# Where the value products and a fill step stand in an attention round on TensorE

## The chip, the cores and the metric

The kernel runs on one NeuronCore of one Trainium2 chip. The metric is the device time of one execution in microseconds (us). Before the change the median of three runs is 2140.48 us (2140.02 to 6885.32).

## The reference

Two blocks follow each other. Attention with 4 sequences, 8 heads, 768 positions and head size 64; each position sees the 128 latest positions and the first 4 ("sinks"). Its output, reshaped to 3072 tokens by 512, goes through 8 experts whose weights come from a Sinkhorn normalisation over all tokens.

```python
scores = scale * np.matmul(q, k.transpose(0, 1, 3, 2))
keep = is_sink | in_window
scores = np.where(keep, scores, -1000000000.0)
a = np.exp(scores - np.max(scores, axis=-1, keepdims=True))
a = a / (np.sum(a, axis=-1, keepdims=True) + 1e-09)
attn = np.matmul(a, v)                      # -> x: 3072 x 512
P = np.exp(x @ w_gate - max); 8 x (rows, columns normalised)
for e in range(E):
    out += P[:, e:e + 1] * (np.maximum(x @ w1[e], 0.0) @ w2[e])
```

## The kernel before, in words

Attention is cut into 48 units: sequence b, block i of 128 query positions (6 per sequence), and half hh of the heads (4 heads, which are two pairs pr = 0, 1). A unit passes through a pipeline of rounds (the loop at L719). In round n TensorE works on four units at once, and on two other things:

- **Scores** of unit n+1 (`scores`, L451): per pair six matmuls, two heads in turn, into one PSUM bank per head (`st0` to `st3`). VectorE adds the mask and takes the maximum (L471), ScalarE takes the exponential (L474), VectorE makes the reciprocal of the sum (L475, L476), GpSimd scales (L478).
- **Values** of unit n-1 (`values`, L511): per pair up to seven matmuls into `O` (L527): three for each of the two key blocks and one for the sinks. After pair 1, `store_x` (L531) copies `O` to `xr`, one half on ScalarE and one on VectorE (both L539), and after hh = 1 stores it.
- **Transposition of q and k** of unit n+2 (`transpose_qk`, L424): four transposes into `st0` (L433), then a high part on ScalarE (L437, `KQ`) and the rest on VectorE (L438, `KQ`).
- **Transposition of the probabilities** of unit n (`transpose_p`, L480): four transposes per pair (two in the first block of a sequence) into `st1` for pair 0 and `st2` for pair 1 (L489). `split` (L348, its instructions have L350) makes the high part `PT` on ScalarE and then the rest on VectorE. The bank is free when VectorE has read it. **Sinks** (`transpose_sinks`, L494) are transposed into `st3` (L506) and copied on ScalarE (L508).
- A **gate step** (`gate_step`): a piece of the logits of tokens that are finished. For the first 1024 tokens this is a group of eight and sixteen matmuls (L568, L577); after that it is one matmul of `gate_tile` (L557), the last of which is followed by a copy on VectorE (L560).
- A **fill step** (`run_fill(1)`, from round 5 on): a piece of the first expert's products. One piece is half of a first product (L606, six matmuls; every second one is followed by L611 on ScalarE and L612 on VectorE) or a part of a second product (L622, three matmuls; at times followed by L628 on ScalarE).

The order on TensorE is written out by hand (`manual_schedule` for TensorE alone); the order of the other engines' queues is set by the tile framework's scheduler from dependencies and program order. Since `st0` to `st3` are one bank each and serve scores, q and k, probabilities and sinks in turn, the scores of pair 0 in the next round (banks `st0`, `st1`) wait for VectorE's reading of the transposed q and k and of pair 0's probabilities, and the scores of pair 1 (`st2`, `st3`) for VectorE's reading of pair 1's probabilities and ScalarE's reading of the sinks.

The kernel's rest (some 1850 us of it) is expert products, which depend on the attention stage's results.

Of the kernel before, what the change touches and what calls it, by code (L numbers as in the profile page):

```python
# [229 lines left out]
def tile_sink_attention_moe(ctx: ExitStack, tc: tile.TileContext, q, k, v, wg, w1, w2, out):  # L230
# [23 lines left out]
    def f32(ap):  # L254
        return ap.bitcast(F32)
# [52 lines left out]
    def split_gate():  # L308
        for kc in range(KC):
            nc.vector.tensor_copy(wgr[:, kc, :], zero)  # L310
        nc.vector.tensor_copy(wgr[:, :, 0:E], wg_raw)
        nc.vector.tensor_sub(wgr[:, :, E:2 * E], wg_raw, f32(wgr[:, :, 0:E]))
        nc.vector.tensor_add(sel, ident[0:2 * E, 0:E], ident[0:2 * E, E:2 * E])
# [54 lines left out]
    def st_tile(shape, k=None):  # L368
        if k is None:
            k, turns[0] = turns[0] % 4, turns[0] + 1  # L370
        return ps_st.tile(shape, F32, name=f"st{k}")
# [30 lines left out]
    def load_sinks(b):  # L402
        vs = seq[b] = att.tile([SK, D], F32, name="vs")
        for r0 in range(0, SK, NK):
            (nc.sync if b else nc.scalar).dma_start(vs[r0:r0 + NK, :], v[b, :, 0:SINK, :])

    def split_sinks(b):

        vm = att1.tile([SK, H, D], F32, name="vm")
        nc.gpsimd.tensor_tensor(vm, seq[b].unsqueeze(1).broadcast_to([SK, H, D]), bd.unsqueeze(2).broadcast_to([SK, H, D]), op=ALU.mult)  # L410
        VS = seq[b] = att.tile([SK, H * D], F32R, name="VS")
        vmf = vm.rearrange("p h d -> p (h d)")
        nc.gpsimd.tensor_scalar(VS, vmf, 1.0, 1.0, op0=ALU.mult, op1=ALU.mult)
        nc.gpsimd.tensor_sub(VS[2 * NK:], vmf[2 * NK:], f32(VS[2 * NK:]))

    def load_block(b, i):
        raws[b, i] = r = [att.tile([P, H, D], F32, name=nm) for nm in ("kr", "qr", "vr")]
        cuts = (0, HH, H) if (b, i) == (0, 0) else (0, H)
        for ts in (((r[0], k), (r[1], q)), ((r[2], v),)):
            for h0, h1 in zip(cuts, cuts[1:]):  # L420
                for t, src in ts:
                    nc.sync.dma_start(t[:, h0:h1, :], src[b, h0:h1, i * P:(i + 1) * P, :].rearrange("h p d -> p h d"))

    def transpose_qk(n):  # L424

        b, i, hh = units[n]
        us[n] = {}
        kr, qr, _ = raws[b, i]
        h0 = hh * HH
        pt = st_tile([P, 4, P], 3 if n == 1 else 0)  # L430
        for pr in range(NP):
            for j, r in enumerate((kr, qr)):
                nc.tensor.transpose(pt[:, 2 * pr + j, :], r[:, h0 + 2 * pr:h0 + 2 * pr + 2, :].rearrange("p h d -> p (h d)"), ident)  # L433
        t = KQ[hh]
        hi, lo = (t[:, w, :, SINK:].rearrange("p r (a c) -> p r a c", a=2)[:, :, :, turn_of(b, i)] for w in range(2))
        src = pt.rearrange("p (r a) t -> p r a t", a=2)
        nc.scalar.copy(hi, src)  # L437
        nc.vector.tensor_sub(lo, src, f32(hi))  # L438
        if i == 1:

            nc.vector.tensor_copy(t[:, :, :, 0:SINK], f32(t[:, :, :, place(b, 0)])[:, :, :, 0:SINK])

    def split_v(n):
        b, i, hh = units[n]
        V = att.tile([P, 2, HH * D], F32R, name="V", bufs=5)
        vs = raws[b, i][2][:, hh * HH:(hh + 1) * HH, :].rearrange("p h d -> p (h d)")
        nc.gpsimd.tensor_scalar(V[:, 0], vs, 1.0, 1.0, op0=ALU.mult, op1=ALU.mult)
        nc.gpsimd.tensor_sub(V[:, 1], vs, f32(V[:, 0]))
        us[n]["V"] = V
# [30 lines left out]
    def transpose_p(n, pr):  # L480

        b, i, hh = units[n]
        u = us[n]
        sc = u["sc"]
        ws = (1,) if i == 0 else (0, 1)
        t = st_tile([P, len(ws), 2, P], 1 + pr)
        for j, w in enumerate(ws):
            for h in range(2):
                nc.tensor.transpose(t[:, j, h, :], sc[:, 2 * pr + h, place(b, i + 1 - w)], ident)  # L489
        PT = att.tile([P, 2, len(ws), 2, P], F32R, name="PT", bufs=5)  # L490
        u["split"] = split(PT, t)
        u["PT", pr] = PT
# [18 lines left out]
    def values(n, pr):  # L511

        b, i, hh = units[n]
        u = us[n]
        if pr == 0:
            u["O"] = ps_o.tile([P, NP, 2, P], F32, name="O")
        cs = slice(pr * P, (pr + 1) * P)
        ops = []
        ws = (1,) if i == 0 else (0, 1)
        for j, w in enumerate(ws):  # L520
            V = us[n - 2 + 2 * w]["V"]
            for x_, y_ in ((0, 0), (0, 1), (1, 0)):
                ops.append((V[:, x_, cs], u["PT", pr][:, y_, j]))
        if i:
            ops.append((seq[b][:, hh * HH * D:][:, cs], u["PS"].unsqueeze(1).broadcast_to([SK, 2, P])))
        for j, (x_, y_) in enumerate(ops):
            nc.tensor.matmul(u["O"][:, pr], lhsT=x_, rhs=y_, start=(j == 0), stop=(j == len(ops) - 1))  # L527
        if pr == NP - 1:
            store_x(n)

    def store_x(n):  # L531
        b, i, hh = units[n]
        u = us[n]
        O = u["O"]
        quads = [(slice(r * D, (r + 1) * D), O[r * D:(r + 1) * D, :, r, :]) for r in range(2)]
        tok = b * S + i * P
        xr = u["xr"] = us[n - 1]["xr"] if hh else att.tile([P, KC, P], F32, name="xr")
        for (rows, o), cp_ in zip(quads, (nc.scalar.copy, nc.vector.tensor_copy)):
            cp_(xr[rows, hh * NP:(hh + 1) * NP, :], o)  # L539
        if hh == 1:  # L540
            nc.sync.dma_start(xscr[:, :, tok:tok + P].rearrange("k p t -> p k t"), xr)
            if tok < NPART:
                g, cols = tok // GT, slice(tok % HT, tok % HT + P)
                for kh in range(2):
                    x_ = xr[:, kh * KH:(kh + 1) * KH, :]
                    b_ = xblock(kh, tok // HT)
                    nc.scalar.copy(b_[:, 0, :, cols], x_)
                    nc.gpsimd.tensor_sub(b_[:, 1, :, cols], x_, f32(b_[:, 0, :, cols]))
                if (tok + P) % GT == 0:
                    later.append(gate_group(g))  # L550
            else:
                later.append(gate_tile(tok // P, xr))
# [28 lines left out]
    def gate_step():  # L581
        if gates and next(gates[0], 0) == 0:
            gates.pop(0)
            gate_step()
# [76 lines left out]
    def run_fill(k_):  # L661
        for _ in range(k_):
            next(fill, None)
# [54 lines left out]
    with tc.manual_schedule(engines={PE}):  # L718
        for n in range(-2, L + 3):  # L719
            on = lambda j: 0 <= j < L  # L720
            if on(n + 2):
                b, i, hh = units[n + 2]
                if hh == 0:
                    with (tc.high_priority() if n == -2 else nullcontext()):
                        load_block(b, i)
                    if i == 0:
                        load_sinks(b)
            if n == -2:
                nc.sync.dma_start(wg_raw, wg.rearrange("(k p) e -> p k e", p=P))
            if n == 2:  # L730
                with tc.issue_after(us[1]["split"][1]):
                    split_gate()
            gates += later
            later.clear()
            if on(n + 1):
                scores(n + 1, 0)
                scores(n + 1, 1)
            if on(n - 1):
                values(n - 1, 0)
            if n >= START:  # L740
                run_fill(1)
            gate_step()
            for j in (0, 1) if n == -2 else (n + 2,) if n >= 0 else ():
                if on(j):
                    transpose_qk(j)
            if on(n):
                transpose_p(n, 0)
                with (tc.issue_after(us[n - 1]["scaled"]) if n > 1 else nullcontext()):
                    split_v(n)
            gate_step()  # L750
            if on(n):
                transpose_p(n, 1)
            if on(n - 1):
                values(n - 1, 1)
            gate_step()
            if on(n) and units[n][1]:
                transpose_sinks(n)
            if on(n) and units[n][1:] == (0, 1):
                with tc.issue_after(us[n]["scaled"]):
                    split_sinks(units[n][0])  # L760
            if n >= START:
                run_fill(1)
            first_w1(n)
        while gates:
            gate_step()
# [760 lines left out]
```

## Time and profile before

| what | before |
|---|---|
| median of the runs | 2140.48 us |
| the profiled execution, its own time | 2140.46 us |
| its span, first to last instruction | 2138.7 us |
| attention rounds in the trace | from about 6 to 300 us |
| granted TensorE clock, mean | 0.997 |

How to read the rows of this document: PE is TensorE, PEld its weight loads, DVE is VectorE, ACT is ScalarE, POOL is GpSimd, SP the queue that issues most DMAs. A row of the timeline gives the start in us from the span's start, the time that it took, engine, source line, operation, what it writes and reads, and how many follow each other; in square brackets the idle time before it and what ended it. A matmul's recorded time covers its whole way through the array, so that matmuls overlap in the record; from one group's start to the next group's start is what a group costs in TensorE's line.

### The profile page before, as it was taken

What the parts mean: (1) busy time and instruction counts of PE and PEld (TensorE: products, weight loads), DVE (VectorE), ACT (ScalarE), POOL (GpSimd) and SP (SyncE); (2) the same over time, 40 slices, a digit from 0 to 9 for tenths busy, and PEclk for the clock granted to TensorE, in tenths of its full rate; (3) what the DMA queues carried; (4) which work ended last, traced back from release to release, by engine and by line L of the source; (5) the groups of instructions that cost most, each with busy time, mean ns of one, the idle gap of its engine ahead of it and who ended that gap; (6) DMA issues with size and microseconds to landing.
All of it is one profiled execution on the core that took longest, in us unless ns stands there. A gap on an engine that the chain in (4) does not pass through costs nothing.

```text
span 2138.7 us, 31819 instructions
## 1 busy us (share of the span) xinstructions
PE 2120.3 (99%) x10501; PEld 1769.8 (83%) x10501; DVE 1538.8 (72%) x2821; ACT 881.9 (41%) x1867; POOL 750.4 (35%) x950
## 2 busy tenths in 40 slices
PE   8999999999999999999999999999999999999998
PEld 7898897888888888888888888888888888888887
DVE  8878868877777776766666666666657666666666
ACT  7777745444444444442333223332333223332322
POOL 7766643233232331232223222233323232233223
PEclk9999999999999999999999999999999999999999
DMA  7434326999999987686666666667866666666662
GB/s 184 95 84 101 86 80 230 314 307 312 294 309 293 310 290 251 216 282 205 204 192 201 208 192 205 203 200 262 297 204 196 199 207 194 200 207 189 205 197 85
DMA packets 397643, 453.83 MB, mean 212 GB/s; under 512 B 99680, under 2 KB 265760, under 8 KB 396576
## 3 DMA queue, kind: packets, MB, share of 16 engines
q1 hardware_dynamic: 397080, 451.57, 68.0%
q8 instruction: 86, 1.41, 0.3%
q14 instruction: 85, 0.70, 0.1%
q10 hardware_dynamic: 392, 0.16, 0.0%
HBM read 314.17 MB, written 137.46 MB: 211 GB/s over the span
## 4 chain that ended last, share of the span: by engine, by line
PE 94%; DVE 3%; ACT 1%; DMA 1%; issue 0%; POOL 0%; SPq 0%; ACTq 0%; DVEq 0%
PE c L791 40%; PE o L1350 20%; PE held L1350 8%; PE held L1035 7%; PE o L1035 7%; PE O L527 3%; PE st L468 2%; PE st L489 1%; PE o L622 1%; PE g L606 1%; ACT sc L474 1%; PE st L433 1%; DVE sc L471 0%; PE O L557 0%; PE st L606 0%
## 5 line engine op out<-in xcount | busy, mean ns | idle before, releaser
L817 ACT CAST hf<-w 128x512 fp32r<-128x512 f32 x448 | 265.0, 620 | 561.5 <-POOL w L1317 299.2
L1350 PE MATMUL o<-hf,W2q 128*128 128x512 f32 x1920 | 472.0, 389 | 0.0
L1350 PEld LDWEIGHTS o<-hf,W2q 128*128 128x128 f32 x1920 | 360.0, 188 | 75.5 <-DVE acc L1364 0.8
L791 PE MATMUL c<-T,W1q 128*128 128x512 f32 x1530 | 389.0, 389 | 0.2 <-DVE w L1298 0.2
L818 DVE TENSOR_TENSOR hf<-w,hf 128x512 fp32r<-128x512 f32 x448 | 330.4, 766 | 74.3 <-ACT hf L817 66.8
L791 PEld LDWEIGHTS c<-T,W1q 128*128 128x128 f32 x1530 | 286.7, 188 | 60.9 <-DVE w L1298 1.2
L1364 DVE TENSOR_TENSOR acc<-o,acc 128x512 f32<-128x512 f32 x298 | 204.6, 687 | 171.5 <-PE o L1350 171.5
L791 PE MATMUL c<-B,W1q 128*128 128x512 f32 x1134 | 278.3, 389 | 0.0
L1317 POOL TENSOR_TENSOR w<-w 128x512 f32<-128x512 f32 x64 | 82.7, 1292 | 493.2 <-DVE w L1299 486.6
L791 PEld LDWEIGHTS c<-B,W1q 128*128 128x128 f32 x1134 | 212.5, 188 | 44.0
L1298 DVE TENSOR_TENSOR w<-c,M 128x512 f32<-128x512 f32 x192 | 132.3, 689 | 138.8 <-PE c L791 133.1
L1294 ACT COPY M<-c 128x512 f32<-128x512 f32 x192 | 112.7, 587 | 250.4 <-PE c L791 250.3
L1350 PE MATMUL held<-hf,W2q 128*128 128x512 f32 x768 | 194.8, 389 | 0.0
L791 PE MATMUL c<-T,W1f 128*128 128x512 f32 x672 | 171.2, 390 | 0.2
L1035 PE MATMUL held<-W2f,h 128*128 128x512 f32 x672 | 171.1, 390 | 0.0
L1035 PE MATMUL o<-W2f,h 128*128 128x512 f32 x672 | 170.6, 389 | 0.1
L1350 PEld LDWEIGHTS held<-hf,W2q 128*128 128x128 f32 x768 | 144.0, 188 | 29.9
L1332 POOL TENSOR_TENSOR w<-w 128x512 f32<-128x512 f32 x64 | 105.7, 1651 | 176.2 <-DVE hf L818 176.2
L1035 PEld LDWEIGHTS o<-W2f,h 128*128 128x128 f32 x672 | 126.0, 188 | 27.0 <-DVE acc L1042 0.9
L791 PEld LDWEIGHTS c<-T,W1f 128*128 128x128 f32 x672 | 125.7, 188 | 27.1 <-ACT M L998 0.5
L1035 PEld LDWEIGHTS held<-W2f,h 128*128 128x128 f32 x672 | 125.8, 188 | 26.4 <-DVE W2f L818 0.5
L844 POOL TENSOR_TENSOR r<-r 128x256 f32<-128x256 f32 x27 | 20.1, 744 | 359.6 <-ACT M L998 210.0
(216 smaller groups left out, 3100.3 us busy)
## 6 DMA issues: line engine op xcount, KB each, us to landing
W2q<-w2s SPq DMA_DIRECT2D x448, 256.0 KB, 3.2
W1q<-w1s SPq DMA_DIRECT2D x444, 256.0 KB, 2.8
w1s<-W1f SPq DMA_DIRECT2D x56, 896.0 KB, 7.6
w2s<-WT SPq DMA_DIRECT2D x136, 256.0 KB, 3.4
r<-in_moe_w_dram SPq DMA_DIRECT2D x64, 512.0 KB, 4.0
w2s<-W2f SPq DMA_DIRECT2D x56, 256.0 KB, 4.8
PB<-psd SPq DMA_DIRECT2D x16, 512.0 KB, 4.2
w2s<-W2f SPq DMA_DIRECT2D x56, 128.0 KB, 6.5
```

Source lines behind the costliest of these rows:

```text
L468: nc.tensor.matmul(ps[h], lhsT=Q[r0:r0 + D, a, pr, :], rhs=K[r0:r0 + D, c, pr, :], start=(j == 0), stop=(j == 2))
L527: nc.tensor.matmul(u["O"][:, pr], lhsT=x_, rhs=y_, start=(j == 0), stop=(j == len(ops) - 1))
L791: nc.tensor.matmul(ps, lhsT=w1(a, k), rhs=x[:, b, k, :], start=(start and j == 0), stop=(stop and j == len(TERMS) - 1), skip_group_check=n ...
L817: nc.scalar.copy(dst[:, 0], src)
L818: at(1, lambda: nc.vector.tensor_sub(dst[:, 1], src, f32(dst[:, 0])))
L1035: nc.tensor.matmul(o, lhsT=h[c, th][:, a, off:off + P], rhs=W2F[n][:, w, c, :], start=(begin and c == 0 and j == 0), stop=(end and c == 1 ...
L1294: nc.scalar.copy(t, T["c2"])
L1298: nc.vector.tensor_add(w, T["c1"], T[m])
L1317: nc.gpsimd.tensor_sub(S3, T["A11"], T["A21"])
L1332: at(k, lambda: nc.gpsimd.tensor_sub(T["A11"], w, T["A11"]))
L1350: nc.tensor.matmul(o, lhsT=W2Q[part, n, m][:, a, k * P:(k + 1) * P], rhs=F[part, n, H_OF[m]][:, w, :], start=(j == 0 and (begin or not hol ...
L1364: nc.vector.tensor_add(sums[m, k], o, sums[m, k])
```

## The change

In the loop over rounds, three things move. Both value products of unit n-1 are now issued together, right behind the scores (before, pair 1's stood behind the transposes of the probabilities). The transposition of q and k comes next, and the first fill step and the first gate step, which stood ahead of it, come behind it. The third gate step, which stood ahead of the sinks, comes behind them. No instruction is added or removed.

```diff
             if on(n - 1):
                 values(n - 1, 0)
+                values(n - 1, 1)
+            for j in (0, 1) if n == -2 else (n + 2,) if n >= 0 else ():
+                if on(j):
+                    transpose_qk(j)
             if n >= START:
                 run_fill(1)
             gate_step()
-            for j in (0, 1) if n == -2 else (n + 2,) if n >= 0 else ():
-                if on(j):
-                    transpose_qk(j)
             if on(n):
                 transpose_p(n, 0)
...
             if on(n):
                 transpose_p(n, 1)
-            if on(n - 1):
-                values(n - 1, 1)
-            gate_step()
             if on(n) and units[n][1]:
                 transpose_sinks(n)
...
+            gate_step()
             if n >= START:
                 run_fill(1)
```

TensorE, in a round of the fourth sequence (of the kind with one gate matmul), from the end of the q and k transposes to the next round's first score matmul. `st_3749` and `st_3760` are the banks of the probabilities of pair 0 and pair 1, `st_3790` that of a score. Before:

```order
L433 MATMUL st_3742<-ident,qr 128x128
L489 MATMUL st_3749<-ident,sc 128x128 x4
L489 MATMUL st_3760<-ident,sc 128x128 x4
L527 MATMUL O<-PT,V 128x256 x6
L527 MATMUL O<-PS,VS 128x256
L506 MATMUL st_3781<-ident,SS_170 96x128
L622 MATMUL o<-W2f,h_2790 128x512 x3
L468 MATMUL st_3790<-KQ_174 128x260
```

The same place after the change (the banks of the probabilities are now `st_3759` and `st_3770`); seven value products (L527) stand no longer between the probabilities' transposes and the next scores, and a fill step (L606) and a gate step (L557) stand between q and k's transposes and theirs:

```order
L433 MATMUL st_3742<-ident,qr 128x128
L606 MATMUL g_3639<-B_131,W_3614 128x256 x2
L606 MATMUL g_3639<-B_130,W_3614 128x256 x2
L606 MATMUL g_3639<-B_131,W_3614 128x256 x2
L557 MATMUL O<-wg_raw,xr 128x8
L489 MATMUL st_3759<-ident,sc 128x128 x4
L489 MATMUL st_3770<-ident,sc 128x128 x4
L506 MATMUL st_3781<-ident,SS_170 96x128
L622 MATMUL o<-W2f,h_2804 128x512 x3
L468 MATMUL st_3790<-KQ_174 128x260
```

The seven L527 that have left this stretch stand right behind the scores now, with the other seven.

VectorE in the same round, from the last reciprocal of the softmax to the first mask and maximum (L471) of the next round. Before:

```order
L476 RECIPROCAL st<-st 128x2
L612 SCALAR_TENSOR_TENSOR h_3621<-g_3622,h_3621 128x256
L438 TENSOR_TENSOR KQ_174<-st_3742,KQ_174 128x2x2x128
L350 TENSOR_TENSOR PT<-st_3749,PT 128x512
L350 TENSOR_TENSOR PT<-st_3760,PT 128x512
L539 COPY xr<-O 64x256
L471 ISA sc,st<-st_3790,mask_79 128x260
```

After:

```order
L476 RECIPROCAL st<-st 128x2
L539 COPY xr<-O 64x256
L438 TENSOR_TENSOR KQ_174<-st_3742,KQ_174 128x2x2x128
L612 SCALAR_TENSOR_TENSOR h_3638<-g_3639,h_3638 128x256
L560 COPY Xt<-O 128x8
L350 TENSOR_TENSOR PT<-st_3759,PT 128x512
L350 TENSOR_TENSOR PT<-st_3770,PT 128x512
L471 ISA sc,st<-st_3790,mask_79 128x260
```

The copy of `O` (L539) has moved from behind the two splits of the probabilities (L350) to ahead of q and k's split (L438); the gate's copy (L560), which stood ahead of the last reciprocals, stands ahead of the splits. ScalarE's line changes in the same way: its copy of `O` now stands between the exponentials and q and k's cast, where it stood behind the casts of the probabilities.

## The prediction

> **What bounds the kernel now.** First the page, for its span and the busy times, then the busy time by stretches of 30 us.
>
> ```profile
> span 2138.7 us, 31819 instructions
> PE 2120.3 (99%) x10501; PEld 1769.8 (83%) x10501; DVE 1538.8 (72%) x2821; ACT 881.9 (41%) x1867; POOL 750.4 (35%) x950
> ```
>
> ```profile
> 0.00:30.00 30.00, 23.38 (x124) 18.46 (x125) 25.57 (x97) 19.74 (x60) 23.49 (x65) 0.89 0.78 193
> 210.00:240.00 30.00, 29.75 (x251) 26.16 (x251) 25.31 (x91) 22.33 (x71) 21.30 (x49) 1.00 0.42 98
> 240.00:270.00 30.00, 29.19 (x245) 25.85 (x244) 25.83 (x88) 22.65 (x72) 19.51 (x44) 1.00 0.33 81
> ```
>
> The columns behind the stretch's length are PE, PEld, DVE, ACT, POOL, then the granted clock. TensorE is busy almost always, also in the rounds of attention, but a matmul's row covers its way through the array, and a wait can hide under the row of the matmul ahead of it. VectorE has 25.3 us of work in 30 us there, so it is a close second. What ends the waits must therefore be read from one round, by the starts of TensorE's groups. This is a round with one gate matmul in which no weight is split:
>
> ```profile
> 212.97 0.97 PE L527 MATMUL O<-PT,V 128*128 128x256 f32 x6
> 213.90 0.87 PE L606 MATMUL g<-B,W 128*128 128x256 f32 x6
> 214.61 0.28 PE L557 MATMUL O<-wg_raw,xr 128*128 128x8 f32 x2
> 214.75 0.31 PE L433 MATMUL st<-ident,kr 128*128 128x128 f32 x1
> 214.98 1.92 POOL L478 TENSOR_SCALAR sc<-sc,st 128x260 f32<-128x260 f32 x4 [2.01 <-ACT sc L474]
> 215.22 1.04 PE L489 MATMUL st<-ident,sc 128*128 128x128 f32 x8
> 215.57 0.56 ACT L437 CAST KQ<-st 128x512 fp32r<-128x512 f32 x1
> 215.71 0.41 DVE L612 SCALAR_TENSOR_TENSOR h<-g,h 128x256 fp32r<-128x256 f32 x1
> 216.01 0.96 PE L527 MATMUL O<-PT,V 128*128 128x256 f32 x6
> 216.03 1.06 ACT L350 CAST PT<-st 128x512 fp32r<-128x512 f32 x2
> 216.16 0.69 DVE L438 TENSOR_TENSOR KQ<-st,KQ 128x512 fp32r<-128x512 f32 x1
> 216.77 1.28 DVE L350 TENSOR_TENSOR PT<-st,PT 128x512 fp32r<-128x512 f32 x2
> 216.96 0.94 PE L622 MATMUL o<-W2f,h 128*128 128x512 f32 x3
> 217.84 0.99 PE L468 MATMUL st<-KQ 64*128 64x260 f32 x12
> 218.08 0.43 DVE L539 COPY xr<-O 64x256 f32<-64x256 f32 x1
> 218.61 0.43 DVE L471 CUSTOM_DVE_ANT_0 sc<-st,mask 128x260 f32<-128x260 f32 x1
> 218.75 0.50 PE L527 MATMUL O<-PT,V 128*128 128x256 f32 x2
> ```
>
> I count a round from the first value product to the next round's first one: 212.97 to 218.75, 5.78 us. TensorE's groups follow without a hole: the scores take 0.91 (217.84 to 218.75) with no stop in the middle. But the reserve is thin. The scores of pair 1 need the bank that VectorE's second split of the probabilities reads. That split ends at 216.77 + 1.28 = 218.05, and the second half of the scores starts at about 217.84 + 0.46 = 218.30. A round in which the split came too late shows what it then costs:
>
> ```profile
> 204.96 1.27 DVE L350 TENSOR_TENSOR PT<-st,PT 128x512 fp32r<-128x512 f32 x2
> 206.28 0.43 PEld L468 LDWEIGHTS st<-KQ 64*128 64x128 f32 x6 [0.18 <-DVE PT L350]
> 206.85 0.98 PE L527 MATMUL O<-PT,V 128*128 128x256 f32 x6
> ```
>
> The splits end at 206.23, the second half of the scores starts at 206.28, and the value products at 206.85: 0.62 us from the end of the splits to the next round's mark. By this, the undisturbed round's splits ended at 5.08 us after its mark, and 5.08 + 0.62 = 5.70 is all that VectorE's line asked for, against TensorE's 5.78. So the round is TensorE's by 0.08 us.
>
> **The change, part by part.** No instruction comes or goes, so TensorE's own work per round stays 5.78 us here. What changes is what stands between the transposes of the probabilities (L489) and the scores that need their banks back. Before, a value product of 0.93 us (212.97 to 213.90), the sinks and a fill step covered the casts and splits; after it only the sinks, at times a gate step, and the fill step do. The transposes themselves start later by that same product.
>
> The new round, from its mark, by the rows above: both value products 2 x 0.93 = 1.86; q and k's transposes 0.47 (214.75 to 215.22); the fill step 0.71 (213.90 to 214.61); the gate matmul 0.14 (214.61 to 214.75). That is 3.18 when the transposes of pair 0 begin. For their end and the start of the cast I take a round in which the two pairs are apart:
>
> ```profile
> 196.53 0.27 PE L433 MATMUL st<-ident,qr 128*128 128x128 f32 x1
> 196.64 0.60 PE L489 MATMUL st<-ident,sc 128*128 128x128 f32 x4
> 196.84 0.58 ACT L437 CAST KQ<-st 128x512 fp32r<-128x512 f32 x1
> ```
>
> ```profile
> L350 DVE TENSOR_TENSOR PT<-st,PT 128x512 fp32r<-128x512 f32 x46 | 29.4, 680 | 0.0
> L350 ACT CAST PT<-st 128x512 fp32r<-128x512 f32 x46 | 25.5, 587 | 0.3
> L350 DVE TENSOR_TENSOR W<-r,W 128x512 fp32r<-128x512 f32 x4 | 2.8, 712 | 0.1
> ```
>
> Four transposes take 0.60 to their end (3.78); ScalarE starts 0.04 behind a transpose's end (196.80 to 196.84: 3.82); the cast takes 0.59 (4.41); VectorE starts 0.03 behind a cast (216.13 to 216.16: 4.44); two splits take 1.28 (5.72); and 0.62 leads to the next mark: **6.34 us**. ScalarE and VectorE are free by then: in the round shown VectorE was through with q and k's split at 216.77, 3.80 after the mark, and the copy of 0.43 that now stands ahead of it makes 4.23, below 4.44. So the loop through the transposes sets the new round, where TensorE set the old one.
>
> What each kind of round loses follows from its time before. Marks from the chain of waits (it puts them 0.07 later, all alike):
>
> ```profile
> 50.89 1.03 PE O L527 x7
> 56.67 1.03 PE O L527 x7
> 71.07 1.03 PE O L527 x7
> 76.77 1.03 PE O L527 x7
> 153.80 1.03 PE O L527 x7
> 169.66 1.03 PE O L527 x7
> 218.82 1.03 PE O L527 x7
> 224.96 1.03 PE O L527 x7
> ```
>
> - Nine rounds with one gate matmul: 6.34 - 5.78 = 0.56 each, 5.0 us. (Two of them hold a weight split and wait already; I take them whole.)
> - Twelve rounds with three gate matmuls, 6.14 before (218.82 to 224.96). The second of them stands between the pairs and is covered by the first pair's cast, so the loop is 6.34 again: 0.20 each, 2.4 us.
> - Five rounds of the first 1024 tokens without a gate matmul, 5.70 before (71.07 to 76.77). The loop is 6.34 - 0.14 = 6.20: 0.50 each, 2.5 us.
> - Rounds 5 to 8, whose fill steps are both first products, 5.78 before (50.89 to 56.67): 0.42 each, 1.7 us.
> - Three times three rounds at a sequence's start. Their transposes and value products are partly halved, they took 15.86 for three (153.80 to 169.66), and VectorE's line sets them rather than the transposes. There the copy of 0.43 that now stands ahead of the splits is added: 9 x 0.43 = 3.9 us. Rounds 3 and 4, without fill steps, likewise: 0.9 us.
> - Two rounds with the gate's group have some 2.9 us of gate matmuls, a third of them now ahead of the next scores; they cover the splits, and cost nothing. Without that cover they would lose 0.5 each.
>
> The sum is 16.4 us. The moved store of `xr` goes out some 3 us earlier on SP's queue, past the loads of k and q; it is read only after attention, and costs nothing. Pair 1's value product, moved forward, needs that pair's splits, which the scores ahead of it have waited for already. Late scores delay the exponentials and GpSimd's scaling; its results (216.90 here, 3.93 after the mark) are needed only by the next round's transposes, 3.18 after the next mark, so this delay is covered by more than 5 us. After the stage TensorE's line is dense, and what starts later ends later.
>
> Bounds. The 0.62 could be 0.46, the scores' second half alone: then the loop is 6.18, and the rounds give 3.6 + 0.5 + 1.7 + 1.0 = 6.8, with the 4.8 of the other rounds at nothing. I take 0.62, since it is measured at this very place. Upward, twelve weight splits of about 0.71 stand on VectorE's line in these rounds; where they came before into 0.08 of reserve or into a round that waited anyway, they may now come whole: at most 8.5 more. And 0.15 more per round at an unseen handover would be 4. So the forecast's own range is +7 to +29.
>
> **The rivals.**
>
> *The old cover was no cover: the whole product is lost.* If the old loop had no reserve at all from the transposes on, each of the thirty full rounds would lose 0.93, and the other eleven 0.43: 32.6 us, 2173. For it speaks that 5.70 and 5.78 are close. Against it: VectorE began the old splits at 3.80 because q and k's split was in its way, not because the transposes were late.
>
> *The copy's new place helps more than the transposes' new place hurts (not slower).* Before, the copy of 0.43 at 218.08 stood between the splits and the next mask and maximum at 218.61, so the whole softmax starts late. With it gone the exponentials start earlier, and rounds that VectorE's line sets (the nine at a sequence's start and the one that ended at 206.85) win 0.43 each: 2136. It decides only if the splits start by about 3.9 after the mark in spite of the later transposes. Against it: the transposes end at 3.78, and a cast must follow.
>
> *No change.* If the casts of the two pairs and the splits follow faster when VectorE and ScalarE stand ready, the loop might come out at 5.78 or less: 2140.5. It would have to lose 0.56 of a chain in which each piece has its measured row.
>
> *The clock falls.* Each round now has holes on TensorE. In the first 30 us, with 23.38 us busy, the granted clock was 0.89; if it were so in thirty rounds, 190 us of TensorE work would take 12% longer, 23 us on top: 2180. Against it: in 240 to 270, where rounds already waited (29.19 us busy), it was 1.00. [...]
>
> **How the numbers follow.** The forecast has 0.65, the whole product 0.13, no change 0.09, not slower 0.09, the clock 0.04. The profiled execution took 2140.46 us (span 2138.7), and the runs' median is 2140.48, so I add to 2140.5: 2157, with an own range of 2147 to 2169. To leave out no more than 2 in 10, the range reaches to 2139 and 2173. A measurement of this kernel tells about 2%, 43 us, from no change; only the clock rival and what I have not thought of reach that: faster 0.01, within 2% 0.95, slower 0.04.
>
> **What would show it.** In the changed profile a round with one gate matmul should last about 6.3 us from mark to mark, one with three also; the scores should stop in the middle, with weight loads of L468 waiting for VectorE's split of the probabilities (L350) in nearly every round; ScalarE's cast of pair 0 should start about 3.8 after the mark, right behind the transposes; and the stage should end some 16 us later, with the rest unmoved. Rounds of 5.8 us with splits that start at 3.9 would refute the loop; a clock below 1.00 behind 30 us would point to the last rival; a shift that arises after 300 us would show that I looked in the wrong stage.

## The result, and the profile after

| what | before | after |
|---|---|---|
| median of six runs each | 2140.94 us | 2157.68 us |
| the profiled execution, its own time | 2140.46 us | 2155.16 us |
| its span | 2138.7 us | 2153.5 us |
| the round of one gate matmul, mark to mark | 5.78 us | 6.24 us |
| mark of the last full round of attention | 278.94 us | 294.20 us |

The changed kernel takes 1.008 times as long (95% interval 1.0069 to 1.0091), 16.7 us by the medians and 14.7 us by the two profiled executions. One of the six runs before took 6885.32 us; without it the median before is 2140.48 us and the difference 17.2 us. The last full round's mark lies 15.3 us later and the span is 14.8 us longer, so all of it arises in the attention stage, and what comes after only starts later.

The page's busy times would not have told this. Of the changed kernel, the page:

```profile
PE 2128.0 (99%) x10501; PEld 1773.6 (82%) x10501; DVE 1541.3 (72%) x2821; ACT 885.3 (41%) x1867; POOL 752.1 (35%) x950
```

and its busy times by stretches (columns as before the change: PE, PEld, DVE, ACT, POOL, granted clock):

```profile
210.00:240.00 30.00, 29.67 (x245) 26.09 (x245) 23.63 (x84) 21.81 (x67) 15.36 (x38) 1.00 0.41 96
240.00:270.00 30.00, 28.79 (x229) 24.48 (x228) 26.75 (x85) 22.56 (x70) 23.48 (x49) 1.00 0.33 80
```

TensorE's 99% is the same as before, and in 210 to 240 it is "busy" for 29.67 of 30 us while its rounds lose up to half a microsecond each. The number of matmul records fell, from 251 to 245, but the two stretches hold partly other rounds, so that this proves little; what tells is the time from one mark to the next. The clock stayed at 1.00, in every stretch of 30 us from 30 us to the end of the attention rounds.

The round of one gate matmul, in the timeline of the changed kernel, from one mark (225.65) to the next (231.89):

```profile
225.65 0.97 PE L527 MATMUL O<-PT,V 128*128 128x256 f32 x6
226.58 0.88 PE L527 MATMUL O<-PT,V 128*128 128x256 f32 x6
...
227.41 0.27 PE L433 MATMUL st<-ident,kr 128*128 128x128 f32 x1
...
227.77 0.96 PE L606 MATMUL g<-B,W 128*128 128x256 f32 x6
...
228.70 1.07 PE L489 MATMUL st<-ident,sc 128*128 128x128 f32 x8
...
229.37 1.08 ACT L350 CAST PT<-st 128x512 fp32r<-128x512 f32 x2 [0.22 <-PE st L489]
229.99 1.29 DVE L350 TENSOR_TENSOR PT<-st,PT 128x512 fp32r<-128x512 f32 x2
...
230.51 1.46 PE L468 MATMUL st<-KQ 64*128 64x260 f32 x12
...
231.34 0.41 PEld L468 LDWEIGHTS st<-KQ 64*128 64x128 f32 x6 [0.19 <-DVE PT L350]
...
231.89 0.74 PE L527 MATMUL O<-PT,V 128*128 128x256 f32 x4
```

Read it as a chain. The transposes start 3.05 after the mark, ScalarE's cast stands waiting for them (0.22 idle) and starts at 3.72, VectorE's splits run from 4.34 to 5.63, the scores stop in the middle (their group lasts 1.46 where 0.98 was usual), the second half's weights load at 231.34, right behind the splits, and 0.61 after the splits' end comes the next mark. No step of this chain has slack, so a delay in any of them is a delay of the round.

In the chain of waits of the changed kernel both value products are one piece of fourteen matmuls, whose starts are the marks (0.07 late, all alike). The first two rows bound a round with one gate matmul, the last two one with three:

```profile
225.72 1.85 PE O L527 x14
231.96 1.87 PE O L527 x14
238.30 1.87 PE O L527 x14
```

6.24 and 6.34. The table of waits from 60 to 300 us, of the changed kernel:

```profile
PEld st L468 <- DVE PT L350: 12.7, 41, 0.8
```

and of the kernel before:

```profile
PEld st L468 <- DVE PT L350: 11.1, 33, 0.4
```

The columns are us in all, times, longest. This view hardly moved, although the loop is now what sets every round: in the kernel before a weight load often stood idle for up to 0.4 us in rounds that had no hole (0.37 at 217.83), and the matmul's own idle time hides under the long record of the matmul ahead of it: one L468 alone has a record of 0.38 us (32.64 in the changed kernel), where twelve of them without a stop take 0.91 (217.84 to 218.75 in the kernel before). Distances from start to start carry the finding.

One place lost what the prediction had at nothing: the two rounds with the gate's group, 9.32 us each where they had 8.63 and 8.62. In the kernel before, the group's third step (L577) stood behind a value product:

```profile
67.15 0.96 PE L527 MATMUL O<-PT,V 128*128 128x256 f32 x6
67.44 0.67 DVE L573 COPY ls<-O 16x512 f32<-16x512 f32 x1
...
68.16 1.05 PE L577 MATMUL O<-sel,ls 16*128 16x8 f32 x8
```

In the changed kernel:

```profile
71.02 0.27 PE L506 MATMUL st<-ident,SS 128*96 128x128 f32 x1
71.06 0.67 DVE L573 COPY ls<-O 16x512 f32<-16x512 f32 x1
...
71.88 1.02 PE L577 MATMUL O<-sel,ls 16*128 16x8 f32 x8 [0.58 <-ACT PT L350]
```

L577 multiplies what VectorE copies in L573. That copy ends at 71.73, and the matmuls start at 71.88. The profile names ScalarE's cast as the releaser (it ends at 71.81), but in the kernel's text the operand of L577 comes from L573 alone. Before, the value product, in TensorE's line from 67.15 to L577's start at 68.16, covered the copy.

### The profile page after: what moved, and what is told of

Same layout as the page of the kernel before. It is cut to its first block, busy times and chain, and to the rows that moved or that the text cites. A ratio compares the mean times of both kernels' runs of the same rounds, so it can differ in the third digit from the quotient of the medians.

```text
span 2153.5 us, 31795 instructions
## 1 busy us (share of the span) xinstructions
PE 2128.0 (99%) x10501; PEld 1773.6 (82%) x10501; DVE 1541.3 (72%) x2821; ACT 885.3 (41%) x1867; POOL 752.1 (35%) x950
## 4 chain that ended last, share of the span: by engine, by line
PE 93%; DVE 4%; ACT 2%; issue 1%; DMA 0%; SPq 0%; DVEq 0%; ACTq 0%
PE c L790 40%; PE o L1349 20%; PE held L1349 8%; PE held L1034 7%; PE o L1034 7%; PE O L527 3%; PE st L468 2%; PE o L622 1%; ACT sc L474 1%; PE st L489 1%; PE g L606 1%; PE st L433 1%; DVE KQ L438 0%; DVE PT L350 0%; DVE sc L471 0%
## 5 line engine op out<-in xcount | busy, mean ns | idle before, releaser
L1316 POOL TENSOR_TENSOR w<-w 128x512 f32<-128x512 f32 x64 | 82.7, 1292 | 491.8 <-DVE w L1298 491.8
L1331 POOL TENSOR_TENSOR w<-w 128x512 f32<-128x512 f32 x64 | 106.2, 1660 | 176.1 <-DVE hf L817 176.1
L1320 POOL TENSOR_TENSOR w<-w 128x512 f32<-128x512 f32 x64 | 83.8, 1309 | 176.2 <-DVE w L1298 174.8
```

Source lines behind the costliest of these rows:

```text
L1316: nc.gpsimd.tensor_sub(S3, T["A11"], T["A21"])
L1320: nc.gpsimd.tensor_add(T["A21"], T["A21"], T["A22"])
L1331: at(k, lambda: nc.gpsimd.tensor_sub(T["A11"], w, T["A11"]))
```

## The experiments

All were timed beside the kernel before on the same chip. The diffs are against the changed kernel, cut to the order on TensorE. "Mark" is the first value product behind the scores, as above. Rounds are counted by n of the loop, and each lasts from its mark to the next.

**One part alone: both value products ahead, the rest as before.**

```diff
             if on(n - 1):
                 values(n - 1, 0)
                 values(n - 1, 1)
-            for j in (0, 1) if n == -2 else (n + 2,) if n >= 0 else ():
-                if on(j):
-                    transpose_qk(j)
             if n >= START:
                 run_fill(1)
             gate_step()
+            for j in (0, 1) if n == -2 else (n + 2,) if n >= 0 else ():
+                if on(j):
+                    transpose_qk(j)
...
+            gate_step()
             if on(n) and units[n][1]:
                 transpose_sinks(n)
...
-            gate_step()
             if n >= START:
                 run_fill(1)
```

> Only pair 1's value product moves forward; the fill step, the gate steps and q and k's transposes keep the places of before. Theory of the loop (transposes of the probabilities, cast, two splits, bank, scores): the transposes begin as late as in the changed kernel, 3.0 to 3.2 us after the mark, so rounds with one gate matmul last 6.2 to 6.3 and the time is 2155 to 2160. Rival, the new place of the fill step and of q and k's transposes: the time falls back to 2139 to 2143.

Measured: 2165.62 us, 1.0118 of before (1.0103 to 1.0134), more than either theory gave. Rounds of one gate matmul and of three take 6.44. Its timeline:

```profile
233.35 0.98 PE L527 MATMUL O<-PT,V 128*128 128x256 f32 x6
...
236.00 0.31 PE L433 MATMUL st<-ident,kr 128*128 128x128 f32 x1
...
237.30 0.69 DVE L438 TENSOR_TENSOR KQ<-st,KQ 128x512 fp32r<-128x512 f32 x1 [0.39 <-ACT KQ L437]
237.90 1.28 DVE L350 TENSOR_TENSOR PT<-st,PT 128x512 fp32r<-128x512 f32 x2
...
239.79 0.98 PE L527 MATMUL O<-PT,V 128*128 128x256 f32 x6
```

With q and k's transposes behind the fill step (2.65 after the mark), VectorE waits for ScalarE's cast of them, and their split then stands ahead of the probabilities' splits, which start at 4.55 instead of 4.34. This is a second chain that I had not counted. So the rest of the change, q and k's transposes ahead of the fill step above all, does not cost; once the values are early it gives back 8 us by the medians, 6.4 us of it between the marks of round 6 and of the last full round. Round 5 of this run, 7.27 long, also fell into a stretch at a lower clock (0.72 from 40 to 46 us).

**The other part alone: everything but the value product.**

```diff
             if on(n - 1):
                 values(n - 1, 0)
-                values(n - 1, 1)
...
             if on(n):
                 transpose_p(n, 1)
+            if on(n - 1):
+                values(n - 1, 1)
             if on(n) and units[n][1]:
                 transpose_sinks(n)
```

> The other half of the change: q and k's transposes ahead of the fill and gate step, the third gate step behind the sinks, but pair 1's value product behind the probabilities' transposes as before. Theory of the loop: the cover is back, rounds of 5.78, 2139 to 2143. Rival of the fill step's and q and k's place: 2155 to 2160.

Measured: 2143.46 us, 1.0013 (1.0004 to 1.0022), 0.5 above the range that was given and still just slower than before. With pair 1's value product back behind the transposes, rounds take 5.78 and 6.19 (in the kernel before 5.78 and 6.13). Most of what is left is in two rounds with weight splits on VectorE (7.44 where it was 5.76, and 7.33 where it was 6.44), and little elsewhere; why these two got longer was not tried. The move of the value product is what costs.

**The copy of `O` back behind the splits, TensorE's order as changed.**

```diff
-        if pr == NP - 1:
-            store_x(n)
...
             if on(n):
                 transpose_p(n, 1)
+            if on(n - 1):
+                with ExitStack() as behind:
+                    for ins in us[n]["split"] if on(n) else ():
+                        behind.enter_context(tc.issue_after(ins))
+                    store_x(n - 1)
```

> TensorE's order as in the changed kernel, but the copies of the value products (ScalarE and VectorE) are held behind the splits of the probabilities, where they stood before. Theory of the loop: rounds with one gate matmul stay at 6.2 to 6.3; only the nine rounds at a sequence's start give some back, 0.3 to 0.4 each: 2153 to 2158. Rival, the copies' new place ahead of q and k's split on VectorE's line costs the time: 2139 to 2144.

Measured: 2155.09 us, 1.0066 (1.0052 to 1.0079). Its timeline (L537 is here the copy):

```profile
223.83 0.98 PE L527 MATMUL O<-PT,V 128*128 128x256 f32 x6
...
227.58 1.08 ACT L350 CAST PT<-st 128x512 fp32r<-128x512 f32 x2 [0.23 <-PE st L489]
228.20 1.29 DVE L350 TENSOR_TENSOR PT<-st,PT 128x512 fp32r<-128x512 f32 x2 [0.23 <-ACT PT L350]
229.52 0.43 DVE L537 COPY xr<-O 64x256 f32<-64x256 f32 x1
230.11 0.74 PE L527 MATMUL O<-PT,V 128*128 128x256 f32 x4
```

The splits start 4.37 after the mark with the copy behind them as with the copy ahead: VectorE and ScalarE now both stand idle for 0.23 in front of them. The round is 6.28. So in full rounds the copy's place is worth nothing, and the loop through the transposes sets them. At a sequence's start it is different: three rounds of 5.60, 5.25 and 6.09 became 5.43, 4.97 and 5.76, and all nine such rounds together give back 1.5 us. Behind the start of the last sequence three full rounds changed too, by +0.66, -0.55 and +0.25; the other full rounds are at most 0.03 longer than in the changed kernel.

**The last fill step ahead of the transposes too.** If cover behind the transposes is what counts, taking more of it away must cost its whole length.

```diff
             if n >= START:
                 run_fill(1)
+            if n >= START:
+                run_fill(1)
             gate_step()
...
             gate_step()
-            if n >= START:
-                run_fill(1)
```

> The changed kernel with its last fill step too moved ahead of the probabilities' transposes (about 0.75 us more ahead, 0.75 less cover behind). Theory of the loop: 6.24 + 0.75 = 7.0 for a round with one gate matmul, 7.1 with three, 0.75 more in thirty rounds: 2174 to 2186. Rival, TensorE's or VectorE's work per round sets the time: no work was added, 2155 to 2161.

Measured: 2183.69 us, 1.0204 (1.0188 to 1.0219). Its timeline:

```profile
241.06 0.98 PE L527 MATMUL O<-PT,V 128*128 128x256 f32 x6
...
244.84 1.07 PE L489 MATMUL st<-ident,sc 128*128 128x128 f32 x8
245.51 1.08 ACT L350 CAST PT<-st 128x512 fp32r<-128x512 f32 x2 [0.93 <-PE st L489]
246.13 1.29 DVE L350 TENSOR_TENSOR PT<-st,PT 128x512 fp32r<-128x512 f32 x2 [0.93 <-ACT PT L350]
...
248.02 0.74 PE L527 MATMUL O<-PT,V 128*128 128x256 f32 x4
```

The transposes start 3.78 after the mark instead of 3.05, and the round is 6.96 instead of 6.24: 0.73 later, 0.72 longer. The pieces behind (0.67 to the cast, 0.62 to the splits, 1.29, then 0.60) are those of the changed kernel to 0.02. This is the plainest confirmation of the loop. Rounds 38 to 41 lost more against the changed kernel, 1.2 to 1.7 each; the waits and stretches at a lower clock of the last section stand in them.

**The first fill step behind the transposes.** The opposite edit: it gives the cover back, with both value products still ahead.

```diff
-            if n >= START:
-                run_fill(1)
             gate_step()
...
             gate_step()
             if n >= START:
                 run_fill(1)
+            if n >= START:
+                run_fill(1)
```

> The changed kernel with its first fill step (0.7 to 0.8 us) moved from ahead of the probabilities' transposes to behind the sinks. Theory of the loop: the loop asks for 6.24 - 0.80 = 5.44, TensorE's own 5.78 sets the round again, and the copies that stand early and the group's gate step with more cover give some back: 2135 to 2141. Rival of the copies' place (unchanged here): 2155 to 2160.

Measured: 2151.04 us, 1.005 (1.0036 to 1.0064): a miss. Less than half of the loss is back. Its timeline:

```profile
221.70 0.97 PE L527 MATMUL O<-PT,V 128*128 128x256 f32 x6
...
224.54 0.43 DVE L539 COPY xr<-O 64x256 f32<-64x256 f32 x1
225.08 0.68 DVE L438 TENSOR_TENSOR KQ<-st,KQ 128x512 fp32r<-128x512 f32 x1
225.68 1.28 DVE L350 TENSOR_TENSOR PT<-st,PT 128x512 fp32r<-128x512 f32 x2
...
226.87 0.41 DVE L612 SCALAR_TENSOR_TENSOR h<-g,h 128x256 fp32r<-128x256 f32 x1
227.57 0.39 PE L527 MATMUL O<-PT,V 128*128 128x256 f32 x1
```

The loop is out of the way: the splits start 3.98 after the mark. But most rounds of one gate matmul still take 5.87 to 5.92, and at a sequence's start one takes 5.94 where the kernel before had 4.91. (Of the 10.5 us by which the last full round's mark lies behind that of the kernel before, 4.0 are there at the mark of round 6 already, and the fill step's place can matter only from round 5 on; see the end of the next section.) Now VectorE's own line is what is too long: the copy, q and k's split, the two splits, and the fill's L612 stand in one row. This gave a new theory: with cover restored, the copy's early place is what is left to pay. The next run tests it.

**Both: the fill step behind, and the copy behind the splits.** Edits of the last and of the copy's run together.

> e4 and e3 together: first fill step behind the sinks, and the copies of the value products behind the splits. In e4 the loop through the transposes no longer set the round, but it came out at 5.87, with the copy of 0.43 ahead of q and k's split on VectorE's line. Theory, that line then sets e4's rounds: with the copy behind, rounds with one gate matmul go to 5.78, those at a sequence's start win 0.3 to 0.5 each, 2140 to 2147. Rival, e4's loss came from the fill step's place alone: 2149 to 2153.

Measured: 2142.32 us, 1.0008 (0.9999 to 1.0017), no difference from before. Its timeline:

```profile
212.85 0.98 PE L527 MATMUL O<-PT,V 128*128 128x256 f32 x6
...
216.51 1.29 DVE L350 TENSOR_TENSOR PT<-st,PT 128x512 fp32r<-128x512 f32 x2
217.74 0.99 PE L468 MATMUL st<-KQ 64*128 64x260 f32 x12
218.66 0.86 PE L527 MATMUL O<-PT,V 128*128 128x256 f32 x5
```

The splits end at 217.80, before the second half of the scores needs their bank, the scores run through in 0.92, and the round is TensorE's again with 5.81. So both value products may stand ahead, provided that as much stands behind the transposes as before and the copy does not stand in front of the splits. It beats nothing: two rounds that held weight splits in the kernel before are shorter (5.80 for 6.77, 5.78 for 6.35), one at a sequence's start and one just behind such a start are longer (5.86 for 4.91, 8.43 for 7.52). So the round of 5.94 in the last run was not long because of the copy.

**Scores of pair 1 ahead of pair 0's.** The 0.61 from the splits' end to the mark should be the second half of the scores. If their bank is needed first, the whole of the scores stands behind the splits.

```diff
-                scores(n + 1, 0)
                 scores(n + 1, 1)
+                scores(n + 1, 0)
```

> The changed kernel with the scores of pair 1 issued ahead of those of pair 0; the transposes of the probabilities keep their order. Theory of the loop through the banks: the pair whose bank comes free last is now needed first, so nothing of the scores is done ahead of it: the mark comes 1.0 us behind the last split (0.6 before), a round with one gate matmul lasts 6.6 to 6.9, and the time is 2168 to 2178. Rival, VectorE's or ScalarE's amount of work sets the round: 2155 to 2161.

Measured: 2178.88 us, 1.0178 (1.0163 to 1.0194), the rounds as expected, the time 0.9 us above what was. Its timeline:

```profile
242.20 0.98 PE L527 MATMUL O<-PT,V 128*128 128x256 f32 x6
...
246.56 1.29 DVE L350 TENSOR_TENSOR PT<-st,PT 128x512 fp32r<-128x512 f32 x2
247.91 0.99 PE L468 MATMUL st<-KQ 64*128 64x260 f32 x12 [0.76 <-DVE PT L350]
248.83 0.74 PE L527 MATMUL O<-PT,V 128*128 128x256 f32 x4
```

The splits end 5.65 after the mark, as in the changed kernel; from there to the next mark it is 0.98 instead of 0.61, and the round is 6.63. The order of the two halves is worth 0.37 per round.

**The third gate step behind the last fill step.**

```diff
-            gate_step()
             if n >= START:
                 run_fill(1)
+            gate_step()
```

> The changed kernel with the third gate step behind the last fill step. Theory: in the two rounds with the gate's group the third step's matmuls waited for a copy on VectorE (0.6 to 0.7 us of hole); behind the fill step that copy is done, so these two rounds go from 9.32 to about 8.65, all others stay, 2155.5 to 2157. Rival: the 0.69 that these rounds lost lies at the scores, as in the others, and they stay at 9.3.

Measured: 2156.36 us, 1.0074 (1.0059 to 1.009). Its timeline in a round with the gate's group:

```profile
73.51 0.95 PE L622 MATMUL o<-W2f,h 128*128 128x512 f32 x3
73.52 0.67 DVE L573 COPY ls<-O 16x512 f32<-16x512 f32 x1
74.39 1.05 PE L577 MATMUL O<-sel,ls 16*128 16x8 f32 x8
```

With the fill step over the copy the two rounds take 8.51 and 8.49 instead of 9.32, and the other rounds from round 6 on are as in the changed kernel to 0.12. By the rounds that is 1.6 us; the medians differ by 1.3. That these rounds lost their time at this wait is shown. That the wait is for L573, and not for the cast that ends 0.08 us later in the changed kernel, is read from the kernel's text. Rounds 1 to 5 are not as in the changed kernel: the mark of round 6 lies 2.4 us later, and with it the last full round's mark is 0.5 later in spite of the gain.

## Why the prediction was right, and where it was not

The forecast was 2157.0, the median is 2157.68. The sum of 16.4 us stands against 14.7 in the two profiled executions and 16.7 between the medians. That the forecast is so close to the median is in part luck: as the table shows, terms too large by 3.2 us stand against terms too small by 2.0, and the changed kernel's median is 2.5 us above its profiled execution. By its own steps, mark to mark in the two traces:

| step | forecast, us | measured, us |
|---|---|---|
| nine rounds of one gate matmul | 5.0 | 4.5 |
| twelve rounds of three | 2.4 | 1.5 |
| five rounds without gate matmul | 2.5 | 2.5 |
| rounds 5 to 8 | 1.7 | 1.1 |
| nine rounds at a sequence's start | 3.9 | 2.7 |
| rounds 3 and 4 | 0.9 | 1.5 |
| two rounds with the gate's group | 0 | 1.4 |

- **What bounds a round.** "So the round is TensorE's by 0.08 us" held: the splits end 5.63 after the mark where they ended 5.08, 0.55 later, and the round is 0.46 longer, so that a reserve of 0.09 was used up first. The 0.93 of cover cost only half of itself because there was slack on the way, where ScalarE and VectorE had q and k's cast and split in front of them: the transposes start 0.80 later than before (2.25 and 3.05 after the mark), the casts 0.66 (3.06 and 3.72), the splits 0.54. The runs that gave the cover back (5.78 and 5.81) and that took more of it (6.96) show it from both sides.
- **The loop's length, 6.34 forecast, 6.24 measured.** The difference lies ahead of the transposes, which start at 3.05 and not 3.18. I had priced both value products at 0.93; the two together take 1.76 (225.65 to 227.41). q and k's transposes take 0.36 and not 0.47, and the fill step and gate matmul 0.94 and not 0.85. The steps behind came out within 0.04: the cast 0.67 behind the transposes' start, the splits 0.62 behind that, 1.29 for two, and 0.61 to the mark, where 0.62 had been taken over the 0.46 of the scores alone.
- **Rounds of three gate matmuls** came out at 6.34, the step's own number, but by luck. By the step they should last as long as rounds of one, since the second gate matmul was to be covered; they last 0.10 longer (6.34 and 6.24), so it is not wholly covered: the two splits, with their pauses, take 1.36 instead of 1.29. This made up for the 0.10 by which the loop was forecast too long. The term is less than 2.4 since one round that was long before (7.52) got shorter by 0.69, and ten of the others lost 0.20 to 0.22. With the copy back behind the splits that one round takes 7.49, so here the copy's early place helped, as one of the rivals had it.
- **Rounds without gate matmul, and rounds 5 to 8,** mostly last 6.06 to 6.09 where 6.20 was forecast. That the first of these two terms fits (2.5) is luck: one of the five rounds lost 0.73 and the other four 0.38 to 0.47.
- **The copy's place.** The term of 0.43 for each round at a sequence's start was too large. The copy is only about half of what these rounds lose: putting it back gave 1.5 of their 2.7 us, with 0.17, 0.28 and 0.33 in three of them, of 0.34, 0.33 and 0.41 lost. In another, which lost 0.71, it gave nothing. The rest of their loss was not taken apart.
- **The step that failed** is "they cover the splits, and cost nothing", of the two rounds with the gate's group. I looked for what the scores wait for, and not for what the moved gate step itself waits for. Its operand is VectorE's copy L573, and the value product that covered this copy was the one that moved. The row that gave it away stands in the trace of before: L577 at 68.16, 0.05 behind the end of L573 (68.11).
- **Rounds 3 and 4** lost more than forecast (0.53 and 0.99). One of them waits 1.53 us for q and k's split; why that split comes so late there was not tried. Nor is it a fixed price: in the run with the third gate step last they take 6.62 and 6.72, where the changed kernel has 5.87 and 6.62. Rounds 1 and 2, of which the forecast said nothing, took 1.0 more, but their first mark came 0.7 earlier.
- **The rivals.** *Whole product lost*: refuted by 0.46 and not 0.93 per round. *No change*: refuted by the interval. *The copy's new place helps*: refuted for the whole: with the copy back behind the splits most full rounds stay as they are, eight of the nine rounds at a sequence's start are as long or shorter, and the last full round's mark comes 1.7 us earlier. It helped in single rounds (7.49 against 6.83). *The clock falls*: it stayed at 1.00 from 30 us to the end of the attention rounds in the profiled execution of the changed kernel.
- **What stays open.** The six runs of the changed kernel lie from 2155.16 to 2159.26, wider than five of the six of before (2140.02 to 2141.46), and the profiled one is the lowest. So 2 us of the 16.7 between the medians have no place in a trace of this kernel. Where such a difference can arise, the run with the third gate step last shows. In its first 65 us the instructions of TensorE, VectorE, ScalarE and GpSimd come in the changed kernel's order, but the mark of round 6 lies at 49.53 and not at 47.10. So two executions of the same rounds can be 2.4 us apart. Whether the longer ones of the six are of this kind was not traced; their mean clocks (0.997 to 0.999, and 0.997 in the profiled one) do not tell them apart.

## What to carry to other kernels

In an engine that works in the written order, what stands between a producer and the next use of its buffer is cover. Before an instruction group is moved, list what it stood in front of, and measure each of those chains from its start to its next use; here a group of 0.93 us covered two chains, and I had counted one. A loop of several engines is best counted from mark to mark, start to start, since an engine's busy share can stay at 99% while every round waits.

Giving one chain its cover back may only uncover the next one, which here was VectorE's own line.

## What the runs showed of the hardware

Some runs with longer waits on TensorE met a stretch at half the clock (0.50). In the run with the first fill step behind the transposes, the matmul that ended the wait:

```profile
97.38 1.31 PE L468 MATMUL st<-KQ 64*128 64x260 f32 x12 [1.43 <-DVE KQ L438]
```

and the busy times behind it (the sixth column behind the stretch's length is the clock):

```profile
99.00:103.00 4.00, 4.00 (x24) 3.99 (x23) 3.17 (x13) 4.00 (x14) 3.57 (x10) 0.57 0.35 85
```

By single microseconds from 99 the clock was 0.71, 0.50, 0.50, 0.58 and 1.00: about 3.4 us at 0.5, from 99.4 to 102.8. q and k's transposes start 0.21 apart there (99.45, 99.66, 99.87) and 0.11 apart in the round ahead (93.50, 93.61, 93.72). The matmuls of those 3.4 us would then take 1.7 us longer, an estimate from these numbers. In the time less is seen: the round in which the stretch lies took 6.29 us, where the kernel before had 5.79. TensorE had stood idle for 1.43 us, about 2 us before the clock fell. In the run with pair 1's scores first a wait of 2.05 us was followed by such a stretch (0.57 from 282 to 286), with the clock at 1.00 in the 8 us ahead of it.

In the run with both fill steps ahead so were waits of 1.82 and 1.51 us (0.62 from 272 to 274 and 0.53 from 274 to 276 behind the first, 0.85 from 284 to 292 and 0.94 from 292 to 300 around the second). That the gaps brought the fall is not shown, only that it followed them. The length of the gap alone doesn't decide it: the changed kernel has one of 1.53 us, in round 4 (ended at 39.27), longer than the 1.43 and 1.51 above, and its clock stayed at 1.00 (30 to 40 and 40 to 50 us). What else decides was not tried. In the profiled execution of the changed kernel this plays no part from 30 us to the end of the attention rounds.
